# The first head group's keys over SyncE's queue in fp32, with a cast on ScalarE and early turns of a higher rank

## The chip, the core and the metric

The kernel runs as one program on one core of one Trainium2 chip. A core has a matrix engine (TensorE, in the profile PE for matmuls and PEld for the loading of weights), VectorE (DVE), ScalarE (ACT), GpSimd (POOL), SyncE (SP), an on-chip memory of 128 partitions, accumulation banks that the matmuls write (PSUM), and 16 DMA engines that move data between the chip's main memory and the on-chip memory. DMAs are issued by an engine's instruction queue; here POOL issues all loads and SP nearly all stores. The metric is the device time of one execution in microseconds (us), less is better, as the median of some runs.

## The reference

Attention over 8 batches and 12 heads of 448 tokens with 64 numbers each, then a two-layer block on its result. All inputs and the output are fp32.

```python
# q, k, v: (8, 12, 448, 64); w_in: (768, 2048); w_out: (2048, 768)
scores = (q @ k.transpose(0, 1, 3, 2)) / 8
attn = exp(scores - max(scores)); attn = attn / (sum(attn) + 1e-9)
x = (attn @ v).transpose(0, 2, 1, 3).reshape(3584, 768)
h = x @ w_in
out = (h * sigmoid(h)) @ w_out           # (3584, 768) fp32
```

## The kernel before

**Tiling.** The 12 heads of a batch are three head groups of four (HG = 4). A unit is one head group of one batch, so there are 24 units; unit 0 is batch 0, group 0. One load brings a unit's keys (`load_k`, L314 to L317) or queries (`load_q`, L319 to L324) as a tile of 128 partitions (4 heads by 32 rows) and 14 x 64 columns; GpSimd's DMA reads fp32 and writes fp16, so that each such tile is 128x896 fp16. The columns of a tile are 14 tokens (TPP = 14) by 64 numbers. The queries of unit 0 are loaded in two pieces of seven tokens (`PIECES`).

**Turning.** The scores need keys and queries with the 64 numbers along partitions. VectorE does this with 32x32 block transposes of pairs of fp16 read as one fp32 (`turn_k`, L375 to L390: for the groups of batch 0 a transpose of 2 x 3 token columns, a lone one, and another of 2 x 3; `turn_q`, L392 to L405, in place). The turned keys are tiles KT (three buffers); the raw keys are tiles rk (two buffers, `NRK = 2`), so that the third keys wait until the first have been turned.

**Scores and exponentials.** For unit 0 there are four bursts of matmuls (L438, tile s, `BURSTS[0]`): the first takes key chunks 0 and 1 with the first half of the queries, the second the same chunks with the second half, the third chunk 2, the fourth chunk 3 together with rows of unit 1. ACT turns each burst into exponentials with two instructions of 128x896 (L483 for the first two bursts, tile T; L494 for the rest, tile E). Three PSUM buffers for s let PE run at most three such halves ahead of ACT. A unit's row sums and its products with V follow (L544, later L558), VectorE makes the reciprocals (L616, L624, L631) and normalizes into xT (L661). Then the two-layer block: h (L673 with w_in), tanh on ACT (L705), the gate G on VectorE (L740, L749), and the second product with w_out (L673, tiles o and p).

**The order of the work.** It is not written by hand. A planner in the kernel (`Order`, from L111) walks a clock with estimated durations, holds lists of ACT and DVE operations that each have dependencies and a bias, and emits the instructions of all engines in its order of time. Ranks come from the bias (`rank`, L38): -10 or less first, up to 35 next, the rest last; within a rank the smaller of ready time plus bias wins. Loads are planned as a queue of POOL in a written order (L1039 on): `plan_k(0, 0)`, `plan_q(0)` (two pieces), `plan_k(0, 1)`, `plan_q(1)`, `plan_k(0, 2)`, V of batch 0 (four loads), `plan_q(2)`, `plan_k(1, 0)`, `plan_q(3)`, w_in in nine pieces, and so on. Each load also waits until the eighth load before it has landed. `plan_turn` (L1077) makes the turning operations, all with bias 20.

**Filling of PE.** While PE would wait longer than `QUIET`, the planner places matmuls on a tile of zeros (`run_zeros`, L1872, tile z) until the two-layer block begins; the first filling is `FIRST` = 47 units of 128 columns.

**Engines at the start.** SP has no work before the first store, which is far behind the start. ACT's first instruction is the load of its function table; its next is the first exponential.

Of the kernel before, what the change touches and what calls it, by code (L numbers as in the profile page):

```python
# [9 lines left out]
FP16 = mybir.dt.float16  # L10
FP32 = mybir.dt.float32
# [22 lines left out]
def act(n):  # L34
    return n * 0.00087 + 0.13
# [75 lines left out]
class Order:  # L111
# [48 lines left out]
    def step(self):  # L160

        soon = []
        for eng in ("ACT", "DVE"):
            if self.free[eng] > self.now:
                soon.append(self.free[eng])
                continue
            best, urgent = None, None
            for op in self.wait[eng]:
                at = op.ready()
                if at is None:  # L170
                    continue
                if at > self.now:
                    soon.append(at)
                    if op.bias <= -10 and (urgent is None or at < urgent):
                        urgent = at
                elif best is None or (rank(op), at + op.bias) < best[0]:
                    best = ((rank(op), at + op.bias), op)
            if best and best[1].bias >= 0 and eng == "DVE" and urgent is not None:
                if urgent < self.now + self.shy * best[1].busy:
                    continue  # L180
            if best:
                self.wait[eng].remove(best[1])
                self.start(best[1])
                soon.append(self.free[eng])
        if self.free["POOL"] > self.now:
            soon.append(self.free["POOL"])
        elif self.pool:
            op, took, ring, gate = self.pool[0]
            at = 0.0
            if ring is not None:  # L190
                at = ring.when(1)
            if at is not None and len(self.sent) >= LOADS:
                at = max(at, self.sent[-LOADS].done + HOP)
            if at is not None and gate is not None:
                g = gate()
                at = None if g is None else max(at, g)
            if at is not None and at <= self.now:
                self.pool.pop(0)
                if ring is not None:
                    ring.take()  # L200
                self.start(op)
                self.sent.append(op)
                took += DMA_SLOW if len(self.sent) == 3 else 0.0
                few = len(self.sent) < 7
                start = self.now + DMA_START + (0.0 if few else DMA_LATE)
                self.dma_free = max(self.dma_free, start) + took
                op.done = self.dma_free + DMA_TAIL + (0.0 if few else DMA_MORE)
                soon.append(self.free["POOL"])
            elif at is not None:
                soon.append(at)  # L210
        return soon
# [3 lines left out]
def kernel(  # L215
# [9 lines left out]
    nc = tc.nc  # L225

    B, NH, S, D = q.shape
    DM = NH * D
    DFF = moe_w_in.shape[1]
    HG = 4  # L230
    NG = NH // HG
    TPP = S // 32
# [9 lines left out]
    NRK, NRQ = 2, 4  # L242
# [2 lines left out]
    EAGER = 1  # L245
    HALVES = 0
    NEAR, LATE = 0.15, -0.3
    COLD, FIRST, QUIET = 8.5, 47, 0.16
    SHY = 0.5
    AWAIT = 1.0  # L250
    FAR = (NT * B // 4 - 3, NT * B // 4 - 1)
    TWB, SXB = 40, 4
    PIECES = ((0, 7), (7, TPP))
# [9 lines left out]
    NE, NX3, NT_ = 10, 8, 2  # L263
# [6 lines left out]
    sb = ctx.enter_context(tc.tile_pool(name="sb", bufs=1))  # L270
# [40 lines left out]
    def group_of(src, b, hg):  # L311
        return src[b, HG * hg : HG * (hg + 1)].rearrange("h (i g) d -> (h i) (g d)", g=TPP)

    def load_k(b, hg):  # L314
        t = sb.tile([128, TPP * D], FP16, name=f"rk_{b}_{hg}", tag="rk", bufs=NRK)
        nc.gpsimd.dma_start(out=t, in_=group_of(k, b, hg))
        rawk[(b, hg)] = t  # L317

    def load_q(n, g0, g1):  # L319
        b, hg = units[n][:2]  # L320
        if g0 == 0:
            rawq[n] = sb.tile([128, TPP * D], FP16, name=f"rq_{n}", tag="rq", bufs=NRQ)
        cols = slice(D * g0, D * g1)
        nc.gpsimd.dma_start(out=rawq[n][:, cols], in_=group_of(q, b, hg)[:, cols])  # L324
# [47 lines left out]
            in_=moe_w_out[128 * f0 : 128 * f1].rearrange("(f p) m -> p f m", p=128),  # L372
        )

    def turn_k(b, hg):  # L375
        t = rawk[(b, hg)][:].bitcast(FP32).rearrange("p (g i) -> p g i", i=32)
        kt = sb.tile([128, TPP, 32, 2], FP16, name=f"KT_{b}_{hg}", tag="KT", bufs=3)
        KT[(b, hg)] = kt
        pairs = kt.rearrange("p g i e -> p (g i e)").bitcast(FP32)
        pairs = pairs.rearrange("p (g i) -> p g i", g=TPP)  # L380
        high = form(b, hg) == "high"
        full = pairs[:, 2 * high : 2 * high + 12].rearrange("p (c x) i -> p x c i", x=4)
        for x in (0, 2):
            first, count = X_TOK[form(b, hg)][x]
            toks = t[:, first : first + 2 * count].rearrange("p (x c) i -> p x c i", c=count)
            at = int(high and count == 4)
            nc.vector.transpose(out=full[:, x : x + 2], in_=toks[:, :, at : at + 3])  # L387
            if count == 4:
                lone = 12 * (not high)
                nc.vector.transpose(out=pairs[:, lone : lone + 2], in_=toks[:, :, 3 - 3 * at])  # L390

    def turn_q(n, g0, g1):  # L392
        t = rawq[n][:].bitcast(FP32).rearrange("p (g i) -> p g i", i=32)[:, g0:g1]
# [593 lines left out]
    units = []  # L987
# [14 lines left out]
    def plan_k(b, hg):  # L1002
        ld_k[(b, hg)] = od.load(128, 2 * D * TPP, lambda: load_k(b, hg), rk_ring)
# [32 lines left out]
        wout_rows.append(f0)  # L1036
        ld_wout.append(od.load(128 * (f1 - f0), 2 * DM, lambda: load_w_out(f0, f1)))

    plan_k(0, 0)  # L1039
    plan_q(0)  # L1040
    plan_k(0, 1)
    plan_q(1)
# [27 lines left out]
    def plan_turns(upto):  # L1070

        while turned["n"] < min(upto, NU):
            if not plan_turn(turned["n"]):
                return
            turned["n"] += 1

    def plan_turn(n):  # L1077
        b, hg, g0, g1 = units[n]
        if b == B - 1 and not rq_ring.can(1, od.now):
            return False  # L1080
        if (b, hg) not in kt_op:
            if not kt_ring.can(1, od.now):
                return False
            kt_ring.take()
            kt_op[(b, hg)] = od.add(
                Op(
                    "DVE", 0.73, lambda: turn_k(b, hg), [ld_k[(b, hg)]], 20, then=rk_ring.give
                )
            )
        if b == B - 1:  # L1090
            rq_ring.take()
        qt_op[n] = [
            od.add(
                Op(
                    "DVE",
                    0.13 + (g1 - g0) / 30.0,
                    lambda g0=g0, g1=g1: turn_q(n, g0, g1),
                    [load],
                    20,
                    then=rq_ring.give if b == B - 1 else None,  # L1100
                )
            )
            for load, (g0, g1) in zip(ld_q[n], PIECES if n == 0 else ((0, TPP),))
        ]
        return True
# [514 lines left out]
    def qk_at():  # L1620
# [11 lines left out]
        turns += [y for x in ns for y in qt_op.get(x, [None])]  # L1632
        if n < ALONE:
            for x in {0 if c == NCH - 1 else i for c, i in BURSTS[n][c]} if n == 0 and c < 2 else ():
                turns = [kt_op.get(units[0][:2]), *qt_op.get(0, [None] * 2)[x : x + 1]]
            if any(x == NCH - 1 for x, _ in BURSTS[n][c]):
                turns += [kt_op.get(units[n + 1][:2]), *qt_op.get(n + 1, [None])]
        at = when(turns)
# [330 lines left out]
```

## Time and profile before

| what | value |
|---|---|
| median of 3 runs | 380.81 us (380.5 to 380.94) |
| the profiled execution's own time | 380.37 us |
| its span, first to last instruction | 378.6 us |
| PE busy | 372.4 us (98% of the span) |
| DVE busy | 269.7 us (71%) |
| ACT busy | 255.5 us (67%) |
| POOL busy | 84.9 us (22%) |
| bytes read from main memory / written to it | 45.61 MB / 11.01 MB |
| granted clock of PE | 1.000 |
| POOL's DMA of one unit's keys, median from issue to landing | 5.0 us |
| SP's stores of 48 KB, median from issue to landing | 1.6 us |

A busy PE says that matmuls are in its pipeline, not that it runs at its peak: their ends are modelled, and an instruction that waits inside a group makes the group long. What the kernel's start is worth is read from the chain of waits in the first microseconds and from who keeps whom waiting after that, since the share of 98% is a mean over the whole run. The DMA row of the page counts a load at its fp16 size: 34.47 MB in all, where the chip read 45.61 MB and wrote 11.01 MB.

### The profile page before, as it was taken

How to read it: one execution, taken by the hardware profiler on the slowest of the kernel's cores; microseconds unless marked ns; L12 is line 12 of the kernel's file. 1: busy time of each engine (PE TensorE's matmuls, PEld its weight loads, DVE VectorE, ACT ScalarE, POOL GpSimd, SP SyncE). 2: the span in 40 equal slices, each digit the busy share in tenths (PEclk: the TensorE clock that was granted, in tenths of full speed). 3: DMA queues.
4: the chain of work that ended last, by engine and by line, in shares of the span. 5: the costliest groups of instructions: out<-in, count | busy, mean ns of one | idle time of the engine just before them, and what ended most of it. 6: DMA issues, size and time to landing. Idle time of an engine off the chain costs nothing.

```text
span 378.6 us, 9949 instructions
## 1 busy us (share of the span) xinstructions
PE 372.4 (98%) x4024; PEld 191.5 (51%) x4024; DVE 269.7 (71%) x553; ACT 255.5 (67%) x400; POOL 84.9 (22%) x155
## 2 busy tenths in 40 slices
PE   7999999999999999999999999999999999999995
PEld 3367664444444444444444454545555555556663
DVE  3666859899995869995969998898475424446541
ACT  4988874897768787877788777658872238882221
POOL 6652438451007326006423200000000000000000
PEclk9999999999999999999999999999999999999999
DMA  7999999946139948148955421200002331002343
GB/s 120 191 208 210 206 204 186 190 53 98 17 92 124 184 49 124 26 94 116 170 86 73 54 53 34 68 18 0 3 1 59 94 74 26 0 2 59 84 110 83
DMA packets 35854, 34.47 MB, mean 91 GB/s; under 512 B 11872, under 2 KB 35040, under 8 KB 35808
## 3 DMA queue, kind: packets, MB, share of 16 engines
q0 software_dynamic: 25312, 22.82, 40.3%
q1 hardware_dynamic: 10080, 10.53, 10.6%
q8 instruction: 31, 0.51, 0.5%
q10 hardware_dynamic: 416, 0.49, 0.4%
q14 instruction: 15, 0.12, 0.1%
HBM read 45.61 MB, written 11.01 MB: 150 GB/s over the span
## 4 chain that ended last, share of the span: by engine, by line
PE 97%; DMA 1%; ACT 1%; DVE 0%; issue 0%; POOLq 0%
PE p L673 32%; PE h L673 21%; PE f L673 16%; PE s L438 12%; PE a L558 8%; PE o L673 3%; PE a L544 2%; PE a L591 2%; DMA rk<-in_k_dram 1%; ACT T L483 1%; PE z L1872 0%; PE z L673 0%; PE z L544 0%; DVE KT L387 0%; ACT ost L977 0%
## 5 line engine op out<-in xcount | busy, mean ns | idle before, releaser
L494 ACT ACTIVATE E<-s 128x896 f16<-128x896 f32 x164 | 142.0, 923 | 23.7 <-PE s L438 23.6
L673 PEld LDWEIGHTS <-w_in_t 128*128 128x128 f16 (+1 forms) x981 | 61.3, 97 | 45.2 <-issue 8.4
L673 PE MATMUL h<-xT,w_in_t 128*32 128x448 f16 (+2 forms) x834 | 84.0, 333 | 0.0
L344 POOL DMA_DIRECT2D V<-in_v_dram x88 | 48.4, 557 | 52.5 <-PE a L558 32.2
L673 PEld LDWEIGHTS <-G 128*128 128x128 f16 (+1 forms) x637 | 43.4, 97 | 32.4 <-issue 5.2
L977 ACT COPY ost<-p 128x384 f32<-128x384 f32 x52 | 24.9, 479 | 50.4 <-PE p L673 31.9
L705 ACT ACTIVATE th<-h 128x448 f16<-128x448 f32 x67 | 36.6, 546 | 22.8 <-PE h L673 19.1
L673 PE MATMUL p<-w_out_t,G 128*128 128x384 f16 (+1 forms) x343 | 51.9, 326 | 0.0
L438 PE MATMUL s<-rq,KT 32*128 32x448 f16 (+3 forms) x728 | 45.4, 347 | 1.3 <-DVE rq L402 1.0
L983 DVE TENSOR_TENSOR ost<-p,ost 128x384 f32<-128x384 f32 x39 | 21.6, 553 | 31.3 <-PE p L673 14.3
L673 PEld LDWEIGHTS <-S 128*128 128x128 f16 (+1 forms) x330 | 29.5, 98 | 23.5 <-issue 4.2
L673 PE MATMUL p<-D,S 128*128 128x384 f16 (+1 forms) x214 | 37.5, 326 | 0.0
L558 PE MATMUL a<-E,V 128*32 128x448 f16 (+1 forms) x640 | 32.9, 356 | 0.0
L749 DVE SCALAR_TENSOR_TENSOR G<-th,h 128x448 f16<-128x448 f16 (+1 forms) x52 | 28.8, 565 | 4.5 <-ACT th L705 3.9
L324 POOL DMA_DIRECT2D rq<-in_q_dram x25 | 13.8, 553 | 67.3 <-PE s L438 57.7
L661 DVE SCALAR_TENSOR_TENSOR xT<-a,rdn 128x448 f16<-128x448 f32 x46 | 27.0, 618 | 2.7 <-PE a L558 2.0
L438 PEld LDWEIGHTS <-KT 32*128 32x128 f16 (+1 forms) x824 | 12.5, 96 | 30.3 <-issue 28.1
L507 DVE TENSOR_TENSOR T<-T,E 128x1792 f16<-128x1792 f16 x20 | 21.7, 1086 | 3.9 <-ACT E L494 3.8
L876 DVE TENSOR_TENSOR p<-f,p 128x448 f32<-128x448 f32 x15 | 9.4, 624 | 20.4 <-PE f L673 13.5
L673 PE MATMUL f<-sx,tw 128*128 128x448 f16 x102 | 23.5, 352 | 0.0
L507 DVE TENSOR_TENSOR T<-E,E 128x1792 f16<-128x1792 f16 x20 | 21.6, 1082 | 2.5 <-ACT E L494 2.5
L558 PEld LDWEIGHTS <-V 128*32 128x32 f16 (+1 forms) x640 | 13.7, 95 | 18.0 <-issue 10.3
(95 smaller groups left out, 430.2 us busy)
## 6 DMA issues: line engine op xcount, KB each, us to landing
out_dram<-ost SPq DMA_DIRECT2D x194, 48.0 KB, 1.6
rk<-in_k_dram POOLq DMA_DIRECT2D x24, 224.0 KB, 5.0
rq<-in_q_dram POOLq DMA_DIRECT2D x23, 224.0 KB, 5.6
w_out_t<-in_moe_w_out_dram POOLq DMA_DIRECT2D x4, 768.0 KB, 12.5
V<-in_v_dram POOLq DMA_DIRECT2D x42, 64.0 KB, 4.1
V<-in_v_dram POOLq DMA_DIRECT2D x42, 48.0 KB, 4.3
w_in_t<-in_moe_w_in_dram POOLq DMA_DIRECT2D x6, 256.0 KB, 9.0
w_in_t<-in_moe_w_in_dram POOLq DMA_DIRECT2D x3, 512.0 KB, 12.3
```

What stands on the lines that cost most here:

```text
L324: nc.gpsimd.dma_start(out=rawq[n][:, cols], in_=group_of(q, b, hg)[:, cols])
L344: nc.gpsimd.dma_start(out=VT[b][32 * x : 32 * (x + 1), hs, at : at + count, :], in_=v[b, hs].rearrange("h (i g) d -> i h g d", g=TPP)[:, : ...
L438: nc.tensor.matmul(out=pS[p0 : p0 + 32 * (x1 - x0), h % 2, at : at + q1 - q0], lhsT=KT[(b, hg)][32 * h : 32 * (h + 1), key_rows(b, hg, c, ...
L494: nc.scalar.activation(out=E[(n, w)][:, 2 * y : 2 * y + 2, :], in_=pS_t[(n, w, y)][:, :, 0:S], func=AF.Exp, scale=attn_scale,)
L507: nc.vector.tensor_tensor(out=T[n], in0=T[n] if step else E[(n, 0)], in1=E[(n, step + 1)], op=ALU.add,)
L558: nc.tensor.matmul(out=a[32 * h : 32 * (h + 1), 0:S], lhsT=VT[b][k0:k1, HG * hg + h, place(b, hg, c), part - 1 :: 2], rhs=e[k0:k1, h], sta ...
L661: nc.vector.scalar_tensor_tensor(out=x3(b, cc)[:, cc % 3, 32 * g0 : 32 * g1], in0=acc[(n, part)][:, 0:nq], scalar=0.5, in1=rdn_t[n].rearra ...
L673: nc.tensor.matmul(out=out[i : i + cut], lhsT=w[:, i : i + cut], rhs=x, start=start, stop=stop, skip_group_check=True,)
L705: nc.scalar.activation(out=th, in_=h_t[(b, f, t0)][:, 0:n], func=AF.Tanh)
L749: nc.vector.scalar_tensor_tensor(out=dst[:, f, at + lo : at + hi], in0=th_t[(b, f, t0)][:, lo - t0 : hi - t0], scalar=1.0, in1=h_t[(b, f, ...
L977: nc.scalar.copy(out=ost(qd, *OUT[m]), in_=bank(qd, BANK[m]))
L983: nc.vector.tensor_tensor(out=t, in0=bank(qd, BANK[m]), in1=t, op=ALU.add)
```

## The change

The keys of unit 0 leave POOL's queue. SP loads them as fp32, in two DMAs by columns (tokens 0 to 7, then 8 to 13; 128x512 and 128x384 fp32), into a tile that takes the buffer of the tenth E tile, and ACT casts each part to fp16 into the same rk tile as before. POOL's first load is now the first piece of unit 0's queries. The three transposes of unit 0's keys become three operations of the planner, the first of them dependent on the first cast, the other two on the second; the first burst of scores depends on two of them and the first query piece. The turns of units 0 to 3 get the bias -11, which puts them in the first rank; the lone transpose has -10. The first filling of PE is 36 units in place of 47, and the planner's rule for later loads begins one load earlier in its count.

```diff
-                few = len(self.sent) < 7
+                few = len(self.sent) < 6
...
-    COLD, FIRST, QUIET = 8.5, 47, 0.16
+    COLD, FIRST, QUIET = 8.5, 36, 0.16
...
+    FIRST_K = ((0, 8, 3.45), (8, TPP, 4.3))
...
+    first_k = {}
+
+    def load_first():
+        t = sb.tile([128, HG, S], FP16, name="first_k", tag=f"E{NE - 1}", bufs=1)
+        t = t.rearrange("p h s -> p (h s)").bitcast(FP32)
+        rawk[(0, 0)] = sb.tile([128, TPP * D], FP16, name="rk_0_0", tag="rk", bufs=NRK)
+        for g0, g1, _ in FIRST_K:
+            first_k[g0] = t[:, D * g0 : D * g1]
+            nc.sync.dma_start(out=first_k[g0], in_=group_of(k, 0, 0)[:, D * g0 : D * g1])
+
+    def cast_first(g0, g1):
+        nc.scalar.copy(out=rawk[(0, 0)][:, D * g0 : D * g1], in_=first_k[g0])
...
-    def turn_k(b, hg):
+    def turn_k(b, hg, parts=(0, 2, 3)):
...
-            nc.vector.transpose(out=full[:, x : x + 2], in_=toks[:, :, at : at + 3])
+            if x in parts:
+                nc.vector.transpose(out=full[:, x : x + 2], in_=toks[:, :, at : at + 3])
             if count == 4:
                 lone = 12 * (not high)
-                nc.vector.transpose(out=pairs[:, lone : lone + 2], in_=toks[:, :, 3 - 3 * at])
+                lone = pairs[:, lone : lone + 2], toks[:, :, 3 - 3 * at]
+        if 3 in parts:
+            nc.vector.transpose(out=lone[0], in_=lone[1])
...
-    plan_k(0, 0)
+    od.emit(load_first)
+    rk_ring.take()
+    cast_op = []
+    for g0, g1, at in FIRST_K:
+        come = Op("SP", 0.0, None)
+        come.done = at
+        fn = lambda g0=g0, g1=g1: cast_first(g0, g1)
+        cast_op.append(od.add(Op("ACT", act(D * (g1 - g0)), fn, [come], -10)))
     plan_q(0)
...
+    def turn_bias(n):
+        return -11 if n <= 3 else 20
...
+        if n == 0:
+            kt_ring.take()
+            for part, busy, x in ((0, 0.37, 0), (2, 0.33, 1), (3, 0.2, 1)):
+                fn = lambda part=part: turn_k(0, 0, (part,))
+                then = rk_ring.give if part == 3 else None
+                kt_op[("part", part)] = od.add(
+                    Op("DVE", busy, fn, [cast_op[x]], -11 + (part == 3), then=then)
+                )
+            kt_op[(0, 0)] = kt_op[("part", 3)]
...
-                    "DVE", 0.73, lambda: turn_k(b, hg), [ld_k[(b, hg)]], 20, then=rk_ring.give
+                    "DVE", 0.73, lambda: turn_k(b, hg), [ld_k[(b, hg)]], turn_bias(n), then=rk_ring.give
...
-                    [load],
-                    20,
+                    [load, *([kt_op[("part", 2)]] if n == 0 and g0 else [])],
+                    turn_bias(n),
...
-                turns = [kt_op.get(units[0][:2]), *qt_op.get(0, [None] * 2)[x : x + 1]]
+                turns = [kt_op.get(("part", i)) for i in (0, 2)]
+                turns += qt_op.get(0, [None] * 2)[x : x + 1]
```

In the order of instructions that the planner makes, PE's work differs in the sizes and places of fillings alone (one of them now stands ahead of the first product with V, which takes over its bank). On ACT two casts stand ahead of the first exponential. On VectorE the lone transpose of a unit's keys comes behind both others in the whole program; the turn of the first query piece stands between the first two key transposes; the turn of unit 2's queries stands ahead of unit 0's first normalization, and the turn of unit 3's keys ahead of its second. SP has its two loads ahead of its first store; POOL has one load less, and the rest in the same order.

More of the change, by code (lines that the diff above doesn't have):

```diff
@@ L373, in load_w_out @@
         )
-    def turn_k(b, hg):
+    def turn_k(b, hg, parts=(0, 2, 3)):
         t = rawk[(b, hg)][:].bitcast(FP32).rearrange("p (g i) -> p g i", i=32)
-        kt = sb.tile([128, TPP, 32, 2], FP16, name=f"KT_{b}_{hg}", tag="KT", bufs=3)
-        KT[(b, hg)] = kt
-        pairs = kt.rearrange("p g i e -> p (g i e)").bitcast(FP32)
+        if (b, hg) not in KT:
+            KT[(b, hg)] = sb.tile(
+                [128, TPP, 32, 2], FP16, name=f"KT_{b}_{hg}", tag="KT", bufs=3
+            )
+        pairs = KT[(b, hg)].rearrange("p g i e -> p (g i e)").bitcast(FP32)
         pairs = pairs.rearrange("p (g i) -> p g i", g=TPP)
@@ L1080, in plan_turn @@
             return False
+        if n == 0:
[5 more added lines that the diff above has]
+                    Op("DVE", busy, fn, [cast_op[x]], -11 + (part == 3), then=then)
+                )
+            kt_op[(0, 0)] = kt_op[("part", 3)]
         if (b, hg) not in kt_op:
```

## The prediction

> **What bounds the kernel now.** I read the page first, for the engine that sets the whole; then the chain of waits in the first 7 us, where the change lies; then ACT's order of time, the DMA traffic, and the places where PE next meets a landing. The page says that PE is the bound:
>
> ```profile
> PE 372.4 (98%) x4024; PEld 191.5 (51%) x4024; DVE 269.7 (71%) x553; ACT 255.5 (67%) x400; POOL 84.9 (22%) x155
> ...
> PE 97%; DMA 1%; ACT 1%; DVE 0%; issue 0%; POOLq 0%
> ```
>
> PE owns the chain apart from a small start. That start, from the chain of waits (start us, length us, what):
>
> ```profile
> 1.25 3.77 DMA rk<-in_k_dram
> 5.02 0.02 issue
> 5.04 0.38 DVE KT L387
> 5.42 0.12 DVE KT L390
> 5.55 0.26 DVE KT L387
> 5.81 0.30 DVE rq L402
> ...
> 6.15 0.63 PE s L438 x16
> 6.78 0.90 ACT T L483
> ```
>
> One load of keys takes 3.77 us, its turns and the first queries' 1.08, and at 6.15 the first scores start; PE has only zeros before. Next, ACT in order of time:
>
> ```profile
> 0.74 1.28 ACT L483 ACT_TABLE_LOAD   x1 [0.74 <-PEq L1953]
> 6.76 3.35 ACT L483 ACTIVATE T<-s 128x896 f16<-128x896 f32 x4 [4.74 <-PE s L438]
> 9.97 9.86 ACT L494 ACTIVATE E<-s 128x896 f16<-128x896 f32 x12
> 20.34 3.35 ACT L494 ACTIVATE E<-s 128x896 f16<-128x896 f32 x4 [0.51 <-PE s L438]
> ```
>
> Sixteen exponentials run without a gap from 6.76 to 19.83, one per 0.8 us: there ACT paces PE through the score buffers, and from 20 us PE is dense. So every tenth by which the first exponential comes earlier is a tenth for the whole kernel, as long as the loads keep up. Whether they do is the second question. DMA by stretches (the last two columns: share of 16 engines, GB/s counted at fp16 size, half of what is read):
>
> ```profile
> 2.00:2.50 0.50, 0.50 (x3) 0.15 (x1) 0.38 (x2) 0.03 (x1) 0.50 (x2) 1.00 0.00 0
> 2.50:3.00 0.50, 0.50 (x2) 0.15 (x1) 0.00 (x0) 0.00 (x0) 0.50 (x2) 1.00 0.81 54
> 3.00:3.50 0.50, 0.50 (x2) 0.15 (x1) 0.00 (x0) 0.00 (x0) 0.50 (x2) 1.00 0.83 125
> 3.50:4.00 0.50, 0.50 (x3) 0.22 (x2) 0.00 (x0) 0.00 (x0) 0.50 (x2) 1.00 1.02 161
> 4.00:4.50 0.50, 0.50 (x4) 0.23 (x3) 0.00 (x0) 0.00 (x0) 0.08 (x1) 1.00 1.12 190
> ...
> 20.00:30.00 10.00, 10.00 (x221) 6.79 (x218) 6.82 (x16) 8.11 (x11) 5.25 (x9) 1.00 1.18 209
> ```
>
> No byte moves before 2.5; from then the engines never rest until after 56 us (205 to 209 GB/s). The tightest later meeting is the last part of w_out (start, length, engine):
>
> ```profile
> 56.39 1.31 PE L673 MATMUL o<-w_out_t,G 128*32 128x384 f16 x28
> 56.49 1.09 POOL L344 DMA_DIRECT2D V<-in_v_dram  x2 [2.36 <-DMA w_out_t<-in_moe_w_out_dram]
> ```
>
> It was issued at 44.33 and took 11.9 us, so it landed at 56.2, and PE used it at 56.39: 0.18 us of cover. PE can be early there by no more than the whole stream of loads is early, plus 0.18. The gain is therefore the smaller of two: x, by which the scores start earlier, and d + 0.18, where d is the stream's lead.
>
> **The keys' path.** Removed: 3.77 us from POOL's issue at 1.25. Added: two SP loads, of 262 and 197 KB. SP is released by the same barrier as ACT (first instruction 0.74), so I put the issues at 0.75 and, after the 0.36 us that a 128-row store occupied SP, at 1.15. No SP load is in this trace. SP's stores give the bounds: a 192 KB one alone took 1.9 us, eight of 48 KB between 57 and 62 us, beside POOL's loads, took
>
> ```profile
> DMA to landing us min/median/max: 2.9/4.7/5.8
> ```
>
> so the second part lands between 1.15 + 1.9 = 3.05 and 1.15 + 5.8 = 6.95. In between I go by the traffic. For a store issued at 365.30 the DMA share is 0.00 until 366.1 and 0.86 after, a start of 0.8 us, so bytes flow from 1.55. In fp32, the first four half microseconds of traffic above carried 54, 125, 161 and 190 KB. On that curve part one (262) is through at 2.8; part two then shares with POOL's queries (229 KB, from 2.6), 688 KB in all, through at 3.95. The 192 KB store leaves 1.9 - 0.8 - 0.6 (at 323 GB/s) = 0.5 us behind its bytes; POOL's keys (459 KB, through at 4.3, landed 5.02) leave 0.7. So part one lands at 3.3, part two at 4.4, the queries at 4.65.
>
> The casts: ACT's copy of 128x384 takes 0.48, its 128x896 exponentials 0.92, hence 0.59 for 512 columns. The first (3.3 to 3.9) and the first transpose (0.38) lie under the wait for part two. On the path are the second cast (4.4 to 4.9), the queries' turn (4.67 to 5.04, beside it) and the second transpose of 0.34: it starts at about 4.97 and ends at 5.31, PE starts at 5.35. x = 6.15 - 5.35 = 0.8. With part two at 3.05 the queries' turn decides; at POOL's own shortest 3.6 us the queries land at 4.85, so x = 0.55, while with queries at 4.2 x is 1.2. At 6.95, x is about -1.75.
>
> **What else moves.** ACT is idle for 4.74 us before the first exponential, so both casts are hidden but for the second's place in the path. The borrowed E buffer is next written after nine other E tiles. The lone transpose (0.20) now comes after 5.3, and the third keys, behind it in POOL's queue with V and unit 2's queries behind them, are issued 0.29 us after it (5.81 to 6.10 before): about 5.8. Queued loads cover that: before, the queries ahead of them landed only at 9.83. Uncovered, each tenth would delay d. POOL's other early loads go out one issue (0.68 us) sooner.
>
> PE's first filling shrinks from twelve matmuls to nine. Before, weight loads for zeros came every 0.43 us until 3.93, then closer; nine end near 4.4, and the idle stretch to 5.35 is 0.95 us against 1.02 before. I cost it at nothing; a burst of 0.63 us at the slow pace would cost 0.4.
>
> The turns' new rank: VectorE stands in order, so unit 0's first normalization now waits for unit 2's queries (landed 15.72), the second for unit 3's keys (16.88). With x and d near 0.8 they have landed (14.9 and 16.1) when VectorE arrives (15.1 and 16.35). With d = 0, the second would end at 16.88 + 0.75 + 0.62 = 18.25 where PE, 0.8 early, wants its bank at 17.9: a cost of at most 0.35. V's last part (landed 14.62, used 14.71) moves with d; a wait of some tenths there is absorbed by the score bursts behind it, which wait for ACT.
>
> **The stream's lead.** Bytes flow at 1.55 where they flowed at 2.6: 1.05. Against it, fp32 traffic on SP's queue used 10.6% of 16 engines for 10.53 MB, 61 us per MB, and POOL's 40.3% for 45.6 MB read, 54; 0.459 MB cost 3.3 engine-us more, 0.2 us over 16. d = 0.85, the cap 1.03, and x = 0.8 is the smaller. The profiled execution took 380.37, so it would take 379.6; it lay 0.44 below the median of 380.81, from which the change gives 380.0.
>
> **Rivals.** *A capped lead.* The bytes in front of the scores are the same, on the same engines; if the two queues only share them, what is saved is POOL's issue of the keys, 0.68 us, less part two's waiting behind queries: 0.1 to 0.7, at 0.4 a time of 380.4. For it: the first traffic ran at 54 to 125 GB/s while only keys were queued, so the engines, not the issue, may be slow at first. Against it: nothing at all flows before 2.5. The Trainium skill ("DMA: Bandwidth & Descriptors", Issuing engines are not separate DMA queues) speaks against the change in this way: DMAs started by several engines run on the same 16 and interleave, and starting them on several saves only the time of initiating them. By that rule alone the time would be 380.81 - 0.68 = 380.1.
>
> *A late second part, slower.* SP's stores beside POOL's loads took a median of 4.7 us against 1.6 over the whole run. If part two, beside queries and keys of POOL, takes as long, it lands at 5.85, its cast ends at 6.35, PE starts at 6.75: 0.6 late, or 381.4, and at 5.8 us 1.75 late, 382.6. It decides from a landing after 5.2. Against it: those stores met a full stream, these loads an empty one.
>
> *More than I count.* If the early slowness is met before the queries come, these land by 4.2, x = 1.2, and the cap of 1.03 decides: 379.8.
>
> **Chances.** The forecast, x of 0.5 to 1.0, has 0.68; the larger lead 0.10; the capped one 0.11; the late part 0.11. A measurement of this kernel can tell about 0.2%, 0.76 us, from no change. I put 0.50 of the forecast above that, since d leaves x room and x can grow where queries land early, and 0.18 below. Faster is 0.50 + 0.10 = 0.60, same 0.18 + 0.11 = 0.29, slower 0.11. The likeliest case alone spans 379.6 to 380.3. The range reaches to a lead of 1.6 (the cap with the early slowness gone too: at the later 418 KB per us the traffic up to 4.5 would have taken 0.6 less) and to 0.1 later than before, which leaves most of the late part out: 379.2 to 380.9.
>
> **What would show it.** First scores at 5.35 rather than 6.15 and the first exponential at 5.95; sixteen exponentials without a gap again; casts near 3.3 and 4.4; the last w_out landing near 55.4 with PE at 55.6. Scores early and the w_out product waiting would mean the cap; a second cast after 5.2, the late part; a gap on VectorE ahead of a normalization, the rank. I am wrong if the scores come early and a later stage gives it back, or if POOL's loads start later beside SP's.

## The result and the profile after

The changed kernel takes 381.59 us (median of 9 runs, 381.42 to 382.0) where the kernel before takes 380.8 beside it (380.36 to 380.98): a ratio of 1.0026, with a 95% interval of 1.0018 to 1.0035. It is slower by 0.79 us between the medians, and by 0.7 to 1.3 us by the interval; the prediction was 0.8 faster. The profiled execution took 381.75, its span is 380.0 (378.6 before). I write "before" and "after" for the two kernels, and "tail" for the time from the end of the last matmul to the end of the span.

The page of after, engines and chain:

```profile
PE 372.2 (98%) x4024; PEld 191.3 (50%) x4024; DVE 269.9 (71%) x553; ACT 256.7 (68%) x402; POOL 84.5 (22%) x154
...
PE 94%; DMA 3%; POOL 1%; DVE 1%; issue 0%; ACT 0%; POOLq 0%
```

PE's work is the same to 0.2 us, but the chain now holds 3% of DMA and 1% of POOL. The chain of waits in the first 8 us says which (start us, length us, what):

```profile
1.26 4.08 DMA rq<-in_q_dram
5.34 0.02 issue
5.36 0.41 DVE rq L421
5.77 0.26 DVE KT L404
6.03 0.14 DVE KT L409
6.17 0.02 issue
6.19 0.02 POOLq L317
6.21 0.49 issue
6.70 0.53 POOL rk L317
7.24 1.24 POOL V L358 x2
```

The chain no longer goes from the turns into PE's scores. It goes from the first queries' landing at 5.34 through their turn, the second and the lone transpose of the keys, into POOL's issue of the third keys at 6.70 (6.10 before) and of V behind it. ACT in order of time:

```profile
3.54 0.62 ACT L331 CAST rk<-first_k 128x512 f16<-128x512 f32 x1 [1.52 <-DMA first_k<-in_k_dram]
4.40 0.51 ACT L331 CAST rk<-first_k 128x384 f16<-128x384 f32 x1 [0.24 <-DMA first_k<-in_k_dram]
6.70 3.35 ACT L502 ACTIVATE T<-s 128x896 f16<-128x896 f32 x4 [1.79 <-PE s L457]
9.91 6.79 ACT L513 ACTIVATE E<-s 128x896 f16<-128x896 f32 x8
17.08 3.35 ACT L513 ACTIVATE E<-s 128x896 f16<-128x896 f32 x4 [0.38 <-PE s L457]
21.48 3.35 ACT L513 ACTIVATE E<-s 128x896 f16<-128x896 f32 x4 [1.06 <-PE s L457]
```

The two casts are where the prediction put them, but the first exponential starts at 6.70, 0.06 earlier than before, and the sixteen that followed one another without a gap are now broken at 17.08 (0.38), and the next gap is 1.06 (0.51 before). DMA by stretches (last two columns: share of 16 engines, GB/s), after and then before:

```profile
2.50:3.00 0.50, 0.50 (x2) 0.15 (x1) 0.00 (x0) 0.00 (x0) 0.50 (x2) 1.00 0.97 367
4.00:5.50 1.50, 1.08 (x4) 0.26 (x2) 0.52 (x2) 0.67 (x2) 0.00 (x0) 1.00 0.95 116
7.50:9.00 1.50, 1.33 (x19) 0.62 (x19) 0.00 (x0) 1.50 (x3) 1.50 (x3) 1.00 0.87 125
9.00:15.00 6.00, 5.53 (x66) 1.97 (x63) 2.95 (x9) 5.94 (x9) 4.60 (x9) 1.00 1.28 169
```

```profile
4.00:5.50 1.50, 1.13 (x6) 0.32 (x4) 0.46 (x3) 0.00 (x0) 0.08 (x1) 1.00 1.23 178
7.50:9.00 1.50, 1.44 (x21) 0.62 (x19) 0.25 (x1) 1.50 (x3) 1.50 (x3) 1.00 1.08 192
9.00:15.00 6.00, 5.82 (x71) 1.95 (x72) 2.80 (x9) 6.00 (x9) 4.65 (x9) 1.00 1.33 183
```

The bytes do start sooner, but the traffic is thinner than before's at 4.0 to 5.5 (116 against 178 GB/s) and at 7.5 to 9.0 (125 against 192), where before had the third keys and V in its queues; between the two, at 5.5 to 7.5, it is 177 against 163. Where PE meets it (PE in order of time, then VectorE):

```profile
15.60 0.56 PE L563 MATMUL z<-T,V 128*32 128x448 f16 x8 [0.50 <-DMA V<-in_v_dram]
...
19.86 0.94 PE L563 MATMUL a<-E,V 128*32 128x448 f16 x16 [0.36 <-DVE xT L680]
```

```profile
18.53 0.64 DVE L404 STREAM_TRANSPOSE KT<-rk 128x192 f32<-128x192 f32 x2 [0.95 <-DMA rk<-in_k_dram]
19.09 0.20 DVE L409 STREAM_TRANSPOSE KT<-rk 128x64 f32<-128x64 f32 x1
19.22 0.59 DVE L680 SCALAR_TENSOR_TENSOR xT<-a,rdn 128x448 f16<-128x448 f32 x1
```

V's last part lands at 15.55 (14.62 before) and PE waits 0.50 for it; unit 3's keys land at 18.51 (16.88), the normalization that now stands behind their turn ends late, and PE waits another 0.36. The same matmuls, compared start by start, lie 0.06 earlier than before at the first scores, 0.89 later at V, 1.15 later at 19 us, and 1.01 later from 30 us to the last. The last matmul ends at 375.71, 1.02 later than before's 374.69.

The span grew by 1.38, so 0.36 is behind the last matmul. There SP's waits differ (engine, line, what it waited for: us in total, times, longest us), from 370 us on, before and after:

```profile
SPq L1964 <- DMA out_dram<-ost: 1.5, 2, 1.0
```

```profile
SPq L2003 <- DMA out_dram<-ost: 1.8, 1, 1.8
```

Before, SP waits twice for stores, and what is left to do when the last one lands is short; after, it waits once, at the first of them. The programs say why. SP's and ACT's transfers signal eight semaphores in turn, and SP's last instructions wait for the eight in their fixed order, 0.062 us each once they are there. With two more transfers the last two stores signal the first and second of the eight in place of the seventh and eighth, so six more waits stand behind the last landing: 6 x 0.062 = 0.37, and the tail is 4.27 instead of 3.91.

### The profile page after: what moved, and what is told of

It reads as the page before. It is cut to its first block, busy times and chain, and to the rows that moved or that the text cites. A ratio compares the mean times of both kernels' runs of the same rounds, so it can differ in the third digit from the quotient of the medians.

```text
span 380.0 us, 9951 instructions
## 1 busy us (share of the span) xinstructions
PE 372.2 (98%) x4024; PEld 191.3 (50%) x4024; DVE 269.9 (71%) x553; ACT 256.7 (68%) x402; POOL 84.5 (22%) x154
## 4 chain that ended last, share of the span: by engine, by line
PE 94%; DMA 3%; POOL 1%; DVE 1%; issue 0%; ACT 0%; POOLq 0%
PE p L692 32%; PE h L692 21%; PE f L692 16%; PE s L457 10%; PE a L577 8%; PE o L692 3%; DMA rk<-in_k_dram 2%; PE a L563 2%; PE a L610 2%; DMA rq<-in_q_dram 1%; POOL V L358 1%; PE z L692 0%; DVE KT L404 0%; POOL rq L338 0%; POOL rk L317 0%
```

## The experiments

Eighteen runs, grouped by what they test (two of them repeat a kernel). One table holds what the text uses: when the third keys were issued, when V's last part landed, when the first scores started and how long the tail was, in the profiled execution, which is one of 5 to 12 (the slowest of them in a1, e3 and e5, the fastest in f4, h3 and h6); then the median beside that of before on the same chip, and the measured ratio with its interval, which is not the quotient of the two medians.

| kernel | third keys | V landed | scores | tail | median / before | ratio |
|---|---|---|---|---|---|---|
| before | 6.10 | 14.62 | 6.15 | 3.91 | | |
| after | 6.70 | 15.55 | 6.09 | 4.27 | 381.59 / 380.8 | 1.0026 [1.0018, 1.0035] |
| a1, after again | 6.69 | 15.93 | 6.08 | 4.28 | 381.9 / 380.42 | 1.0042 [1.003, 1.0054] |
| e1, old ranks | 6.67 | 15.17 | 6.06 | 4.28 | 381.6 / 380.34 | 1.003 [1.0019, 1.0042] |
| g1, seven more stores | 6.84 | 15.48 | 6.22 | 4.04 | 381.32 / 380.64 | 1.0016 [1.0007, 1.0024] |
| h4, six more stores | 6.35 | 15.75 | 5.74 | 3.91 | 381.23 / 380.5 | 1.0018 [1.0009, 1.0027] |
| e3, keys turned first | 5.53 | 14.22 | 6.30 | 4.27 | 380.45 / 380.34 | 1.0005 [0.9996, 1.0014] |
| e4, third keys free | 3.51 | 14.32 | 5.89 | 4.27 | 380.72 / 380.34 | 1.0012 [1.0003, 1.0021] |
| e7, e3 and old ranks | 5.73 | 14.45 | 5.78 | 4.29 | 380.81 / 380.64 | 1.0005 [0.9996, 1.0014] |
| f4, e7 and long filling | 5.82 | 14.49 | 5.91 | 4.28 | 381.18 / 380.64 | 1.0014 [1.0005, 1.0024] |
| h3, e4 and six stores | 3.51 | 14.43 | 5.49 | 3.91 | 380.34 / 380.5 | 0.9998 [0.999, 1.0007] |
| h6, h3 and old ranks | 3.51 | 13.94 | 5.51 | 3.91 | 380.87 / 380.42 | 1.0007 [0.9999, 1.0016] |
| h5, e3 and six stores | 5.65 | 13.95 | 5.74 | 3.91 | 380.04 / 380.42 | 0.9999 [0.9989, 1.001] |
| i1, h5 again | 5.74 | 14.81 | 5.98 | 3.90 | 380.41 / 380.46 | 0.9996 [0.9984, 1.0008] |
| h1, h5 and old ranks | 5.67 | 14.78 | 6.46 | 3.91 | 380.76 / 380.46 | 1.0003 [0.9991, 1.0016] |
| e2, before and ranks | 5.76 | 15.50 | 6.12 | 3.91 | 380.75 / 380.34 | 1.0011 [1.0002, 1.002] |
| g2, before, two more stores | 6.07 | 14.60 | 6.13 | 4.29 | 381.17 / 380.64 | 1.0017 [1.0008, 1.0025] |
| f3, before, short filling | 5.74 | 15.57 | 5.81 | 3.91 | 380.55 / 380.5 | 1.0006 [0.9997, 1.0015] |
| e5, before, third keys free | 4.04 | 14.95 | 6.14 | 3.89 | 380.53 / 380.42 | 1.0006 [0.9998, 1.0015] |

(e6 is told below.)

### The third keys

e3 moves the first queries' first turn on VectorE behind all three transposes of unit 0's keys, so that these do not wait for the queries:

```diff
-    for _, _, fn in sorted(od.out, key=lambda x: x[:2]):
+    fns = [fn for _, _, fn in sorted(od.out, key=lambda x: x[:2])]
+    fns.remove(qt_op[0][0].emit)
+    fns.insert(fns.index(kt_op[("part", 3)].emit) + 1, qt_op[0][0].emit)
+    for fn in fns:
         fn()
```

> The changed kernel, with the turn of the first query piece moved on VectorE behind all three key transposes. Theory of the loads: the lone transpose ends near 5.5 instead of 6.16, the third keys are issued near 6.0 instead of 6.70, DMA does not dip between 7.5 and 9, and V's last part lands near 15.0 instead of 15.55; PE late by 0.3 to 0.6 us at 26 us; 380.9 to 381.3 us. Rival that SP's fp32 traffic itself makes the stream late: V's last part still lands after 15.4 and the time stays at 381.4 or more. Theory of the ranks: unchanged, 381.5.

e4 keeps the order and gives unit 0's fp16 keys a second borrowed E buffer, so that the third keys wait for no turn:

```diff
-        rawk[(0, 0)] = sb.tile([128, TPP * D], FP16, name="rk_0_0", tag="rk", bufs=NRK)
+        u = sb.tile([128, HG, S], FP16, name="rk_0_0", tag=f"E{NE - 2}", bufs=1)
+        rawk[(0, 0)] = u.rearrange("p h s -> p (h s)")[:, 0 : TPP * D]
...
-    rk_ring.take()
...
-                then = rk_ring.give if part == 3 else None
+                then = None
```

> The changed kernel, with unit 0's fp16 keys in a second borrowed E buffer, so that the third keys' load waits for no turn; all else of the change stays. Theory of the loads: the third keys are issued near 3.6, no dip between 7.5 and 9, V's last part lands by 14.9, PE's wait of 0.50 us for it is gone; 380.3 to 380.9 us. Rival that SP's fp32 traffic itself makes the stream late: V's last part after 15.3, 381.3 us or more. Theory of the ranks: V early, but the waits of PE and ACT near 20 us stay: 381.1 to 381.4.

Two different edits that share only the earlier issue of the third keys, and of V behind them, bring the ratio from 1.0026 to 1.0005 and 1.0012; e3 came out below the 380.9 to 381.3 that was expected of it. After itself, on the chip on which h5, h6 and e5 ran, repeats its lateness:

> After, unchanged, for a second profile and on the same chip as the next three. If the late third keys and the order of the last waits are the cause: third keys issued at 6.3 to 6.8 again, V's last landing above 15, tail 4.27, 0.6 to 1.0 above before. If the 0.79 was chance of the loads: V's last landing near 14.5 and the time near before's.

It came out at 1.0042, with the third keys at 6.69 again and V later still; PE in order of time:

```profile
15.97 0.56 PE L563 MATMUL z<-T,V 128*32 128x448 f16 x8 [1.05 <-DMA V<-in_v_dram]
```

The table shows the pattern over all profiles. In the five kernels of the change that issue the third keys at 6.35 or later, V's last part landed at 15.17 to 15.93; in the nine that issue them by 5.82, at 13.94 to 14.81. The DMA traffic from 7.5 to 9.0 us, where after's was thin, separates the same groups: 96 to 149 GB/s in the five, 168 to 190 in the nine, 192 in before. One of each, h4 with late third keys and h3 with early ones, differ in e4's edit alone and ran on one chip (381.23 and 380.34 us):

```profile
7.50:9.00 1.50, 1.30 (x23) 0.51 (x17) 0.84 (x4) 1.50 (x3) 1.50 (x4) 1.00 0.98 149
9.00:15.00 6.00, 5.52 (x64) 1.87 (x63) 2.60 (x9) 6.00 (x8) 3.89 (x7) 1.00 1.20 157
```

```profile
7.50:9.00 1.50, 1.36 (x18) 0.52 (x12) 0.76 (x3) 1.50 (x3) 0.14 (x1) 1.00 1.05 174
9.00:15.00 6.00, 5.75 (x76) 2.16 (x74) 2.81 (x9) 6.00 (x8) 4.04 (x7) 1.00 1.36 194
```

In h4 POOL issued nothing between 3.5 and 6.35 us, and from 7.5 on the 16 engines ran at 149 GB/s, though two loads issued earlier were still in flight (landed at 7.84 and 8.90). So two queued loads were no cover here: the rate was lower while they were being finished, and V came later. That the same edit does nothing for before, whose third keys go out at 6.10, is the control:

```diff
-        t = sb.tile([128, TPP * D], FP16, name=f"rk_{b}_{hg}", tag="rk", bufs=NRK)
+        if (b, hg) == (0, 0):
+            t = sb.tile([128, HG, S], FP16, name="rk_0_0", tag=f"E{NE - 2}", bufs=1)
+            t = t.rearrange("p h s -> p (h s)")[:, 0 : TPP * D]
+        else:
+            t = sb.tile([128, TPP * D], FP16, name=f"rk_{b}_{hg}", tag="rk", bufs=NRK)
```

> Before, with unit 0's keys in a borrowed buffer, so that the third keys wait for no turn, and nothing else. If the wait for the turn costs only where it lies past about 6.1 us (as in after): within 0.2 of before. If it costs before as well: 0.3 to 0.5 faster than before, and freeing it is then a gain of its own that the change neither made nor spoilt.

1.0006, 0.9998 to 1.0015. On balance freeing the third keys is no gain of its own; it undoes a loss that the change made. (In e5's profile, the slowest of its eleven, the second piece of the first queries landed at 8.08, where it was 6.91 in before, and PE waited 1.3 us for it. f3, whose third keys wait for the turn, shows nearly the same landing, 7.93, so this is not shown to be a price of the edit.) (V can also land late by itself: it did in two of before's variants, e2 and f3, at 15.50 and 15.57, with the third keys at 5.7.)

### The last waits

g2 gives before two transfers more, by splitting two of SP's stores of 32 rows in the middle of the kernel; nothing else changes:

```diff
-            eng.dma_start(out=dst, in_=ost_t[(qd, i, j)][32 * w : 32 * (w + n), :])
+            parts = ((0, 16), (16, 32)) if w == 0 and 0 <= 4 * (qd - 4) + 2 * i + j < 2 else ((0, 32 * n),)
+            for r0, r1 in parts:
+                eng.dma_start(out=dst[r0:r1], in_=ost_t[(qd, i, j)][32 * w + r0 : 32 * w + r1, :])
```

> Before, with two of SyncE's middle stores split, so that two transfers more run ahead of the last store, as in after, and nothing else changes. Theory T: the last store signals the first semaphore instead of the seventh; tail 4.27 us rather than 3.91, time 0.37 above before (ratio 1.0010). Rival L: ratio 1.000, tail 3.9.

The tail became 4.29 and the ratio 1.0017 (1.0008 to 1.0025), 0.3 to 0.95 us for an expected 0.37. g1 and h4 are after with the same splitting for seven and for six stores (`< 7`, `< 6`).

> After, with seven of SyncE's middle stores (32 rows) split into two of 16 rows, so that 9 rather than 2 transfers more than before run ahead of the last store, and that store signals the eighth of the eight semaphores instead of the first. Theory T (tail): SyncE waits for the eight semaphores in their order at 0.062 us each once they have come; after's last store signals the first, so seven waits (0.43 us) stand behind it: this kernel saves 0.43, some 0.35 to 0.4 above before, and in the profile the time from the last matmul's end to the span's end is 3.84 us rather than 4.27. Rival L (the loads alone make the 0.79): no change against after, 0.8 above before, 4.27 us of tail or a tail that varies. Seven more issues of about 0.5 us on SyncE in the middle are taken as free, since nothing waits for them.

> After, with six of SyncE's middle stores split in two, so that eight transfers more than before run ahead of the last two stores and these signal the seventh and the eighth semaphore again, as in before; nothing else changes. Theory T: from the last matmul's end to the span's end 3.91 us as in before (4.27 in after), and the time 0.42 above before (after's 0.79 less 0.37). Rival: 0.8 above before. The other 0.42 would be the third keys' late issue (6.70 us).

g1's tail was 4.04, not the 3.84 that I expected: I had looked at the last store of ACT alone, and with seven the one of SP, issued in the same moment, came round to the first semaphore, so seven waits stood behind that. With six both stand as in before, and the tail is 3.91 exactly. h4's time shows little of it (1.0018), since its V landed at 15.75 and PE waited 1.21 for it. Over the kernels with early third keys it can be seen: the four with a tail of 4.27 to 4.29 (e3, e4, e7, f4) have a mean ratio of 1.0009, the five with 3.9 (h5, i1, h3, h6, h1) 1.0001; the difference is 0.3 us.

### The ranks of the turns

e2 is before with the ranks alone (the bias of units 0 to 3; the lone transpose keeps its old place between the other two); e1 is after with the old ranks; e7, h6 and h1 put the old ranks on kernels with early third keys.

```diff
     def turn_bias(n):
-        return -11 if n <= 3 else 20
+        return -11 if n < 1 else 20
...
-                    "DVE", 0.73, lambda: turn_k(b, hg), [ld_k[(b, hg)]], turn_bias(n), then=rk_ring.give
+                    "DVE", 0.73, lambda: turn_k(b, hg), [ld_k[(b, hg)]] + [lambda: when(norm_of.get(0, [])[1:] or [None])] * (n == 3), turn_bias(n), then=rk_ring.give
```

> The kernel before, with the new rank of the turns of units 0 to 3 alone (keys still one load by POOL). Theory of the loads: unit 2's queries and unit 3's keys land at 15.7 and 16.9 as before, VectorE waits little for them, PE has the bank of the second normalization in time or 0.1 to 0.2 late: 380.7 to 381.0 us. Theory of the ranks: 0.4 to 0.8 us slower, 381.2 to 381.6.

> The changed kernel, with the turns of units 1 to 3 in their old rank and the turn of unit 3's keys held behind unit 0's second normalization, so that on VectorE the turns of unit 2's queries and unit 3's keys stand behind the normalizations again; all else of the change stays. Theory of the loads (the late stream of loads costs the time, the ranks add to it): the 0.36 us in which PE waits for a normalization near 19.5 goes and ACT's gap near 20.5 falls from 1.06 us to about 0.5; PE late by 0.4 to 0.6 us at 26 us rather than 1.0; 381.0 to 381.3 us. Theory of the ranks (the loads' lateness has cover, the ranks are the loss): 380.8 us or less.

> After, with both edits at once: the first queries' first turn behind all three transposes of unit 0's keys (so the third keys are issued near 5.5 rather than 6.70), and the old ranks (bias -11 for unit 0 alone, unit 3's keys turned behind the second normalization). Theory R (the ranks cost 0.4, as the kernel of before with the ranks alone measured): 0.4 under the kernel with the keys turned first alone (380.45 where before was 380.34), so 380.0, or 0.3 under before. Rival: the ranks cost only where the loads are late: 380.4 to 380.5, 0.1 over before.

> After with unit 0's keys in a second borrowed buffer, six stores split, and the old ranks of the turns. Theory: ranks cost nothing once loads are early: -0.1 against before, as h3 (ratio 0.9998), within 0.2. If the ranks alone cost 0.4 (as the kernel of before with them measured): 0.4 under h3, 0.5 under before.

> The kernel before this one in the call, with the old ranks of the turns. If ranks cost nothing once the third keys are early (as the third keys' free kernels showed): within 0.15 of it. If they cost 0.4: 0.4 under it.

e2's 1.0011 looked like a cost of 0.4. But its profile shows PE 0.04 behind before until 14 us and then waiting for a V that landed at 15.50. And in none of the four pairs of the change's kernels did the old ranks win (e1's 381.6 is above both of its expected ranges): 1.003 against after's 1.0026 (e1), 1.0005 against 1.0005 (e7, e3), 1.0007 against 0.9998 (h6, h3), 1.0003 against 0.9996 (h1, i1). The 0.36 for which PE stood behind a normalization in after comes from unit 3's keys landing at 18.51, not from the rank by itself. That the ranks cost nothing where the loads are early is what three of the pairs show, each to about 0.5 us. Why e2's interval lies above 1 is not settled: one late V in one profile does not show that its eleven executions had it.

### The shorter filling

f4 is e7 with the first filling 11 units longer, emitted but not planned, so that nothing else moves (`run_zeros(n + more, wide, i)` with `more = 11`); f3 is before with `FIRST` = 36.

> The kernel before this one in the call, with a first filling of 47 units instead of 36, and nothing else moved on any engine. Theory W (the shorter filling leaves TensorE idle from 5.2 us to its first scores, and in some executions its matmuls then stay at the slow pace, 0.427 us per 512 columns, until about 10 us, which costs 0.5 to 1.0 us there): no execution more than 0.7 us above the fastest, the median lower by 0 to 0.1, and the zeros behind the first scores at 0.22 in the profile. Rival: the filling ends at 6.2 us at the slow pace, behind the turn of the keys, so that scores start later by 0.1 to 0.3 and the median is higher by as much.

> Before, with a first filling of 36 units instead of 47 and nothing else moved. Theory W (a TensorE idle from 5.1 us to its first scores stays at the slow pace in some executions until about 10 us): median 0.1 to 0.3 above before, with executions 0.7 to 1.0 above. Rival, as the prediction had it (the filling costs nothing): ratio 1.000.

f3 came out at 1.0006 (0.9997 to 1.0015) and f4 above e7, not below it, with executions from 380.38 to 382.05: a longer filling does not take the scatter away. Yet PE's pace at the first scores does differ from execution to execution. The first sixteen score matmuls of after, and those of e3, by PE in order of time:

```profile
6.09 0.58 PE L457 MATMUL s<-rq,KT 32*128 32x224 f16 x16 [1.01 <-DVE KT L404]
```

```profile
6.30 0.93 PE L457 MATMUL s<-rq,KT 32*128 32x224 f16 x16 [1.07 <-DVE rq L421]
7.17 1.14 PE L1911 MATMUL z<-zeros 128*128 128x256 f16 x4
8.24 0.93 PE L457 MATMUL s<-rq,KT 32*128 32x224 f16 x16
```

In e3's profiled execution (381.46, the slowest of its eleven) PE ran its early scores at the slow pace, and went from 0.15 behind before at its first scores to 0.82 behind from 10.5 us on, with all loads early. The same pace stands in the profiles of e1 and g1. There PE came to V at 15.54 and 15.67, after its last part had landed, and was 0.61 and 0.75 behind before at 14 us already: in these two profiles the slow scores set the time and the late V was hidden behind them. In the trace's records the full clock is granted from 10.25 us in e3, 10.24 in e1 and 9.82 in g1, and between 3.9 and 7.0 for the first time in all the others. Among these e7 (from 6.80) ran its first sixteen at the slow pace too, in 0.94, and h1 lost the full clock again from 7.91 to 11.32. It is not a matter of the shorter filling alone: g2, with before's 47 units, had the full clock from 7.00 and took 0.93 for its first sixteen.

### The first queries' flight

e6 is before with the two loads of the first queries ahead of the first keys in POOL's queue, and no load on SP.

```diff
+    fns.remove(ld_k[(0, 0)].emit)
+    fns.insert(fns.index(ld_q[0][1].emit) + 1, ld_k[(0, 0)].emit)
```

> Before, with the two loads of the first queries ahead of the first keys in GpSimd's queue, and no load on SyncE: how long the first queries take when they are the first load and nothing runs beside them. If SyncE's two loads are what made them late in after (5.34 us, 4.08 after the issue): they land by 4.5 to 4.8, near the 4.65 of the prediction. If the load is slow by itself: 5.2 or later. The keys land near 5.6, so the kernel as a whole is 0.3 to 0.6 slower than before.

From issue to landing of the two loads, in e6 and in after:

```profile
DMA to landing us min/median/max: 2.8/2.9/2.9
```

```profile
DMA to landing us min/median/max: 4.1/4.3/4.4
```

Alone, in e6's one execution, the first piece lands at 4.16; with SP's two loads beside it at 5.34, and over the 14 profiles of the change's kernels at 4.74 to 5.97, with a median of 5.32. (e6 as a whole took 383.11 against a median of 380.5, since its keys landed at 7.27.) So SP's loads take about 1.2 us from the load that the first scores wait for. The packets by queue say where part of it goes. Until 3.2 us, in after and then in before (queue: packets, MB, share of 16 engines; q1 is SP's, q0 POOL's, and no other queue is listed):

```profile
q1 hardware_dynamic: 233, 0.40, 42.6%
```

```profile
q0 software_dynamic: 22, 0.04, 15.6%
```

In after POOL's queue moves its first byte at 3.23 us, when 0.40 of SP's 0.46 MB have gone; in before and in e6 it does at 2.64, and over the 14 profiles of the change's kernels at 3.10 to 3.31. Why POOL's loads begin to flow 0.6 later beside SP's was not tested.

### Both undone

h3 and h5 are e4 and e3 with the six stores split, i1 is h5 once more.

> The kernel before this one in the call, with unit 0's keys in a second borrowed buffer, so that the third keys wait for no turn (the edit of the kernel with the third keys free). By theory (tail 0.37, third keys' wait 0.4 to 0.55, nothing else): 0.0 against before, -0.15 to +0.1, and third keys issued at 3.5 us, tail 3.91. If a third cost is in the change (ranks, warm-up): 0.3 to 0.5 above before.

> After with the first queries' first turn behind all three turns of unit 0's keys, and six stores split so that the last waits stand as in before. By the sum (tail 0.37, third keys' wait 0.4 to 0.55): 0.0 against before (-0.3 to +0.15), 0.8 under after in this call; V's last landing near 14.3. If the tail's 0.37 does not count in the time: 0.2 to 0.4 above before.

> The kernel with the keys turned first and the last waits as in before, again. If the early start is worth what its profile showed (TensorE 0.41 ahead at its first scores, 0.54 at the end): 0.3 to 0.5 under before, interval below 1. If its executions scatter as before's do about the same middle: ratio 1.000.

All three come back to before's time: 0.9998, 0.9999 and 0.9996, with intervals that all hold 1. Taking the third keys' wait and the last waits away takes the whole loss away, to about 0.1%. In h5's profile PE is 0.41 ahead of before at the first scores and 0.53 at the end, with the exponentials unbroken:

```profile
6.35 3.35 ACT L502 ACTIVATE T<-s 128x896 f16<-128x896 f32 x4 [1.78 <-PE s L457]
9.55 9.86 ACT L513 ACTIVATE E<-s 128x896 f16<-128x896 f32 x12
```

Its median was 0.38 under before's, but the repeat's was 0.05 under. No version was shown to beat the kernel before.

## Why the prediction was wrong

**Right.** PE is the bound; ACT paces it through the first sixteen exponentials; SP's parts land near 3.3 and 4.4 (3.52 and 4.38), the casts take 0.6 and 0.5 and are hidden, and the second ends at 4.91 (4.9 predicted). Where the queries land early, the step from them to the scores holds: in h3 they landed at 4.74, and the scores started at 5.49 with PE 0.66 ahead.

**The size of x was wrong first.** The prediction had "the queries at 4.65", and x = 0.8. They landed at 5.34 and x was 0.06. The step behind 4.65 let the queries' bytes flow from 2.6 beside part two's, had the 688 KB of both queues through at 3.95 on a traffic curve that before had shown for one queue by itself, and landed the queries 0.7 behind that. In the trace POOL's first byte moved at 3.23 and SP's last packet ended at 4.08: POOL's queue did not share from 2.6, it began 0.6 later. The bound that I named for a late queries load, POOL's own shortest flight of 3.6, was no bound (after's flight was 4.08); the median over 14 profiles is 5.32, 0.67 later than 4.65. The page of the Trainium skill that I cited, "DMA: Bandwidth & Descriptors" (Issuing engines are not separate DMA queues), says that transfers of several issuers interleave on the same 16 engines. The two flights, 2.9 alone and 4.1 to 4.4 beside SP's loads, agree with it in kind. But I drew from it only that the gain would be smaller, 380.1, when the interleaving also delays the load that is needed last.

**The step that turned it into a loss is "Queued loads cover that".** The third keys were to be issued "about 5.8" after the lone transpose. The queries' turn stands ahead of that transpose on VectorE, so their lateness moved the transpose's end from 5.5 to 6.17, and the issue came 0.53 after it where I had taken 0.29: 6.70. I had written that uncovered "each tenth would delay d", and took the cover as given because the queries ahead had landed only at 9.83 before. But the loads in flight did not keep the engines full. The traffic at 7.5 to 9.0 fell from 192 to 125 GB/s, V's last part and the loads behind it moved back, and the stream's lead was not 0.85 but a lag: the last w_out landed at 56.77 instead of 55.4 (56.21 before). When the third keys are early the lag goes, but d = 0.85 does not come: the last w_out landed at 54.80 to 56.31 in the nine such profiles, 55.66 in the mean, against 55.80 to 56.21, 55.94 in the mean, in the four profiles with before's order of loads (before, e2, g2, f3). That is a lead of about 0.3, so the term d was mis-sized as well. By mean ratios the late issue costs 0.65 to 0.9 us: 1.0033 (after, a1, e1) against 1.0009 (early, long tail), and 1.0018 (h4) against 1.0001 (early, short tail).

**What I did not look for: the tail.** Nothing in the prediction went past the last matmul. The two loads on SP shift the order in which the last stores are waited for, 0.36 to 0.38 us in every profile of the change whose number of transfers was left alone.

**"I cost it at nothing", the filling.** Right for the median, as f3 and f4 show, but scores at the slow pace are not rare: in three of 13 profiles of the change's kernels with 36 units PE scored slowly until about 10 us, at 0.7 us in e3, where the 0.4 that the prediction set against it was low. As g2 scored slowly with 47 units, the filling is not shown to be the cause.

**The ranks at nothing, 0.35 at most if d = 0.** d was below 0 and the stall was 0.36, at the place named; without late loads they cost nothing that three pairs could find.

**The rival on the slower side** named a late second part, which was not late (4.38; it was to decide from 5.2). The mechanism was the neighbouring one: the load beside it was late. And "POOL's loads start later beside SP's", one line under what would make the prediction wrong, is what took x.

**Still open.** The kernels with both costs undone start their scores at 5.49 to 6.46, 0.3 earlier on average than before's 6.15, and their ratios lie within 0.1% of 1. With x and d both near 0.3 in place of 0.8 and 0.85, little was left to gain. Whether 0.3 us are lost again further on, or are there and too small for executions that scatter over 1 to 2 us, was not settled. It was not tried to bring the queries' landing forward, for instance by less traffic on SP ahead of it.

## What to carry to other kernels

When a load is moved to a second issuer, the loads left on the first are not free of it: ask which of them the next step needs last, and give that one the delay of all that now travels beside it. Count the cover of a late issue in bytes still to move and not in landings still to come, because the rate can fall before the last load lands, as it did here (125 against 192 GB/s). And look behind the last instruction as well: where completions are waited for in a fixed order, two transfers added at the start can cost time at the end.

## What the runs showed of the hardware

The granted clock of PE turned at moments of a fixed grid: in e5's profile it went to full at 5.22, back to half at 8.64 and to full again at 12.05, 3.41 us apart. The place of the grid against the kernel's start differs from run to run. The Trainium skill ("TensorE: Matmul & The Clock Gate", Part 1: The HAM clock gate) has such a free-running window of 3413 ns, and these records agree. They add what a window that is busy in part does. The clock stayed at half after windows in which PE was idle for 0.83 us (e1, g2) or more, and was granted after windows with 0.66 (e4) or less. It was kept after windows with 1.21 and 1.35 us of idle (after, f3) and taken back after 1.59 (h1), 1.67 (e5) and 2.11 (e6). With 36 units of filling the idle stretch ahead of the first scores was 0.26 to 1.5 us (1.02 in before, with 47), and so whether PE was at its pace by then depended on the grid's place.

V's last landing varied by about 1 us with nearly the same issue times (14.6 to 15.6, issued at 8.1 to 8.5, in before, e2, g2 and f3), which is as much as the whole effect of this change.
